# A cached-attention decode kernel: V loads follow K by one head instead of one head and one chunk, and the first loads are split over two issuing queues

## The chip, the cores and the metric

The kernel runs on one core of a Trainium2 chip. The time is the device time of the whole program in microseconds, where smaller is better. Most runs of one kernel agree within 0.3%, which is 8 us here. A program can also run in a slower, disturbed state. Engines are named TensorE (PE in the profile, PEld its weight loads), ScalarE (ACT), VectorE (DVE), GpSimd (POOL) and SyncE (SP). A "load" is a DMA of 4 MB from memory into one of four buffers.

## The reference

One token attends to a cache of 65,536 keys and values in each of 32 heads of 128 numbers (bf16). Beside it runs a small gated feed-forward network, and a scalar gate mixes the two.

```python
g = sigmoid((x * gate_w).sum(-1))
q = x @ wq                                   # 512 -> 32 heads x 128
scores = einsum(q, k_cache) * 128 ** -0.5    # 65536 scores a head
o = einsum(softmax(scores), v_cache)
a = o @ wo
b = (silu(x @ w_gate) * (x @ w_up)) @ w_down
out = g * a + (1 - g) * b
```

K and V are 512 MiB each, so each number is used once: the kernel is a stream from memory with some arithmetic behind it.

## The kernel before

K and V are cut into 128 chunks each, of 4 MB, four chunks to a head. SP loads them into a ring of four buffers in the order of `jobs`. A load may be issued only when the job four places earlier has been used up.

```python
V_LAG = 1
jobs = [("wq", i) for i in range(NQW)]
for s in range(NK):                              # NK = 128, NCH = 4
    jobs.append(("k", s))
    if s == 0:
        jobs += [("wgu", 0), ("wd", 0)]          # (cut) the feed-forward weights
    if s >= NCH + V_LAG:
        jobs.append(("v", s - NCH - V_LAG))
jobs += [("v", s) for s in range(max(0, NK - NCH - V_LAG), NK)]

@block.sync
def _(sp):
    sp.dma_start(xT, x) ...; sp.dma_start(gwT, gate_w) ...     # (cut)
    for job in jobs:
        load(sp, w, job)                         # waits until its buffer is free
```

TensorE works in slots, one for each K chunk. It transposes 96 of the chunk's 128 blocks (of 128 keys each) in 12 groups of eight, ScalarE copies each group out of PSUM (`KT`), and TensorE forms the scores; VectorE does the scores of the other 32 blocks. When a head's four chunks are done, VectorE takes the maximum, POOL reduces it over the partitions and scales it to the bias of the exponential (`nbias`), and ScalarE does one softmax piece per slot. The V chunk belonging to it is multiplied at the end of a later slot.

```python
V0 = NCH + V_LAG                                 # the slot of the first V chunk
# ScalarE, over all groups g:
if g == (V0 - 1 + n_p) * GPC + GPC // 2:         # GPC = 12: in the middle of slot V0-1+n_p
    softmax(n_p); n_p += 1
w("tdone", g + 1)                                # (cut)
nc.scalar.activation(KT[:, g % NKT, :], kt_ps(g), ACT.Copy, ...)

# TensorE
c0 = V0 + 2
for c in range(c0): slot(c, w)                   # unrolled
with nc.Fori(0, turns, 1, ...): ...              # two slots a turn
for c in range(c0 + turns * 2, NK): slot(c, w)   # the last slot
while done_v < NV:                               # the V chunks behind the last K
    if done_v in proj_at: out_proj(*proj_at[done_v])   # before V125 and before V126
    values(done_v, w); done_v += 1
w("s_otl", 1)
mm(psT[0:1, 0, 0:D], oTn[:, H - 1:H], wo_sb[:, H - 1, :], ...)    # the last head

# POOL, behind the last head's maximum and bias
w("s_rs0", 1)
nc.gpsimd.partition_all_reduce(Lt[:, 0:H - 1], rs[:, 0:H - 1], P, RADD)   # denominators of heads 0 to 30
w("s_rs1", 1)
nc.gpsimd.partition_all_reduce(Lt[:, H - 1:H], rs[:, H - 1:H], P, RADD)   # of head 31
```

ScalarE issues one more load at the start, the 4 MB output weights `wo_sb`, as 1 KB pieces. It is needed only at the end.

## Time and profile before

| Quantity | Before | Where it is read |
|---|---|---|
| Time | 2563.13 us, median of 3 runs before the prediction (2559.98 to 2563.48) | runs |
| Span of the profiled run | 2563.3 us | page |
| DMA busy | 0.9 or more in 39 of 40 slices | page, part 2 |
| Busy share of PE, ACT, DVE | 72%, 58%, 49% | page, part 1 |
| Last K chunk in (K127), first transpose | 2498.6 us | timeline |
| Wait of TensorE for the last V chunk (V127) | 1.18 us | chain of waits |

These lines are from the page of the kernel before: the DMA share and the rate in 40 slices, and the chain of work that ended last by engine.

```profile
DMA  9999999999999999999999999999999999999996
GB/s 403 423 425 432 432 431 431 430 431 430 433 430 432 430 431 433 430 433 429 433 429 431 433 426 431 430 432 427 426 425 418 431 429 427 423 422 426 422 419 297
...
DMA 67%; PE 13%; ACT 11%; issue 9%; POOL 0%; DVE 0%; ACTq 0%; SPq 0%; POOLq 0%; DVEq 0%
```

The engines that move data never rest before the last slice, and two thirds of the chain of waits is DMA. Only what moves this stream, or what comes after it, can change the time.

The start and the first head, from the timeline (start in us, duration, engine, line, operation, count; in brackets the idle time before and what ended it):

```profile
0.73 0.39 SPq L286 DMA_DIRECT2D xT<-in_A_x_dram  x1
...
1.64 0.42 SPq L252 DMA_DIRECT2D ring<-in_A_wq_dram  x1
...
19.33 3.55 PE L508 MATMUL psS<-xT,ring 128*128 128x1 bf16 x128 [12.33 <-DMA ring<-in_A_wq_dram]
...
95.84 2.30 POOL L304 PARTITION_ALL_REDUCE amx<-mxs  x1 [81.27 <-DVE mxs L441]
...
105.88 0.26 POOL L306 TENSOR_SCALAR nbias<-amx 128x1 f32<-128x1 f32 x1 [7.74 <-issue]
106.18 0.40 ACT L325 ACTIVATE pcol<-sS,nbias 128x128 bf16<-128x128 f32 x1 [5.44 <-POOL nbias L306]
...
111.05 0.33 SPq L252 DMA_DIRECT2D ring<-in_A_v_cache_dram  x1
...
123.14 0.33 SPq L252 DMA_DIRECT2D ring<-in_A_k_cache_dram  x1
```

The weights are issued third. In slot 4 ScalarE stands still for 5.44 us for the first head's bias, and the loads of V1 and K7 (111.05 and 123.14) are issued late because the buffers are still in use.

The tail is best read in the chain of waits, in order of time (start, duration, what; "issue" is time in which the profile shows no wait, here POOL's own):

```profile
2513.05 0.70 DVE mxs L441
...
2514.33 11.67 issue
...
2526.62 9.41 issue
2536.03 0.65 POOL Lt L309
...
2537.43 6.13 PE psT L596 x15
2543.56 3.31 PE psO L566 x128
2546.87 5.02 PE psT L596 x16
2551.89 3.29 PE psO L566 x128
2555.18 1.18 issue
2556.36 3.55 PE psO L566 x128
...
2560.96 0.74 DVE finrow L493
```

Behind the last head's maximum (2513.05) stand two long POOL steps (11.67 and 9.41 us), then the output projection in two parts with V125 and V126 around them. TensorE is through at 2555.18 and waits 1.18 us for V127. Two things end almost together: the stream, and the chain of work behind K127.

The trace also records 16 completions for every load. They are taken here as one from each DMA engine, which e9 and e10 bear out below; the records do not say which engine each is from. Numbered from 0 in the order of `jobs`, load 258 is V127's first part. The spread between a load's first and last completion grows from 2.5 us at load 0 to 16 us at the end. Of load 257, twelve completions come within 2.8 us, and the last comes 6.6 us after the one before it: one engine lags most. Stretches of the tail show it too (stretch, its length, busy time and count of PE, PEld, DVE, ACT, POOL; then the clock that TensorE was granted, as a share of full speed, the DMA share and GB/s):

```profile
2550.00:2555.00 5.00, 5.00 (x136) 3.77 (x135) 0.00 (x0) 0.00 (x0) 0.00 (x0) 1.00 0.07 31
```

A share of 0.07 is about one engine of 16.

### The profile page before, as it was taken

How to read it: one execution, taken by the hardware profiler on the slowest of the kernel's cores; microseconds unless marked ns; L12 is line 12 of the kernel's file. 1: busy time of each engine (PE TensorE's matmuls, PEld its weight loads, DVE VectorE, ACT ScalarE, POOL GpSimd, SP SyncE). 2: the span in 40 equal slices, each digit the busy share in tenths (PEclk: the TensorE clock that was granted, in tenths of full speed). 3: DMA queues.
4: the chain of work that ended last, by engine and by line, in shares of the span. 5: the costliest groups of instructions: out<-in, count | busy, mean ns of one | idle time of the engine just before them, and what ended most of it. 6: DMA issues, size and time to landing. Idle time of an engine off the chain costs nothing.

```text
span 2563.3 us, 88371 instructions
## 1 busy us (share of the span) xinstructions
PE 1848.0 (72%) x41279; PEld 1701.2 (66%) x41280; DVE 1259.2 (49%) x953; ACT 1484.7 (58%) x1799; POOL 42.3 (2%) x72
## 2 busy tenths in 40 slices
PE   6877777777777767776777677777766776777766
PEld 4777666666666666666766666666666666666665
DVE  2754554554455445544554454455444544455441
ACT  3766665566556655655665566556655665566552
POOL 0000000000000000000000000000000000000000
PEclk8778776777767767777676677777777777777776
DMA  9999999999999999999999999999999999999996
GB/s 403 423 425 432 432 431 431 430 431 430 433 430 432 430 431 433 430 433 429 433 429 431 433 426 431 430 432 427 426 425 418 431 429 427 423 422 426 422 419 297
DMA packets 42053, 1088.43 MB, mean 425 GB/s; under 512 B 4481, under 2 KB 8578, under 8 KB 8706
## 3 DMA queue, kind: packets, MB, share of 16 engines
q1 hardware_dynamic: 37874, 1083.46, 98.8%
q10 hardware_dynamic: 4112, 4.19, 0.5%
q8 instruction: 27, 0.44, 0.1%
q14 instruction: 40, 0.33, 0.0%
HBM read 1087.64 MB, written 0.00 MB: 424 GB/s over the span
## 4 chain that ended last, share of the span: by engine, by line
DMA 67%; PE 13%; ACT 11%; issue 9%; POOL 0%; DVE 0%; ACTq 0%; SPq 0%; POOLq 0%; DVEq 0%
DMA ring<-in_A_k_cache_dram 66%; ACT KT L345 10%; PE psT L535 9%; PE psS L548 2%; PE psO L566 1%; ACT pcol L325 1%; DMA ring<-in_A_wq_dram 1%; PE psT L596 0%; PE psT L515 0%; POOL amx L304 0%; PE psS L508 0%; PE psO L589 0%; DVE mxs L441 0%; ACTq L205 0%; DVE sS L434 0%
## 5 line engine op out<-in xcount | busy, mean ns | idle before, releaser
L345 ACT ACTIVATE KT<-psT 128x1024 bf16<-128x1024 bf16 x1536 | 1443.0, 1039 | 972.7 <-PE psT L535 969.8
L535 PE MATMUL psT<-ident,ring 128*128 128x128 bf16 x12288 | 1138.7, 255 | 527.6 <-DMA ring<-in_A_k_cache_dram 525.5
L535 PEld LDWEIGHTS psT<-ident,ring 128*128 128x128 bf16 x12288 | 912.3, 116 | 538.3 <-DMA ring<-in_A_k_cache_dram 271.7
L424 DVE TENSOR_TENSOR prod<-ring,qbc 128x2048 f32<-128x2048 bf16 x256 | 586.7, 2292 | 592.1 <-DMA ring<-in_A_k_cache_dram 586.7
L548 PE MATMUL psS<-qc,KT 128*128 128x1 bf16 x12288 | 550.8, 166 | 139.9 <-ACT KT L345 92.7
L548 PEld LDWEIGHTS psS<-qc,KT 128*128 128x128 bf16 x12288 | 467.7, 100 | 257.7 <-ACT KT L345 252.5
L426 DVE TENSOR_REDUCE sS<-prod 128x16 f32<-128x2048 f32 x256 | 585.2, 2286 | 8.7
L566 PE MATMUL psO<-pcol,ring 128*128 128x1 bf16 x16384 | 475.7, 164 | 19.9 <-issue 9.2
L566 PEld LDWEIGHTS psO<-pcol,ring 128*128 128x128 bf16 x16384 | 450.4, 99 | 24.0 <-issue 14.6
L434 DVE COPY sS<-psS 128x96 f32<-128x96 f32 x128 | 33.0, 257 | 607.2 <-PE psS L548 607.2
L325 ACT ACTIVATE pcol<-sS,nbias 128x128 bf16<-128x128 f32 x128 | 52.3, 408 | 41.7 <-POOL nbias L306 41.6
L304 POOL PARTITION_ALL_REDUCE amx<-mxs x32 | 16.1, 502 | 2137.5 <-DVE mxs L441 2137.5
L445 DVE COPY oparts<-psO 128x1 f32<-128x1 f32 x127 | 18.9, 149 | 25.2 <-PE psO L566 25.1
L306 POOL TENSOR_SCALAR nbias<-amx 128x1 f32<-128x1 f32 x32 | 24.5, 767 | 333.6 <-issue 333.6
L325 ACT ACTIVATION_READ_ACCUMULATOR pcol<-sS,nbias 128x1 f32 x128 | 26.1, 204 | 0.0
L380 DVE COPY qc<-qTb 128x1 bf16<-128x1 bf16 x128 | 19.9, 156 | 4.4
L441 DVE TENSOR_REDUCE mxs<-sS 128x1 f32<-128x512 f32 x32 | 21.7, 677 | 0.0
L332 ACT ACTIVATE qbc<-psT 128x512 bf16<-128x512 f32 x4 | 2.4, 597 | 23.1 <-PE psT L515 23.1
L596 PE MATMUL psT<-wo_sb,oTn 128*1 128x512 bf16 x31 | 11.2, 540 | 5.6 <-DVE oTn L476 5.6
L508 PE MATMUL psS<-xT,ring 128*128 128x1 bf16 x128 | 3.6, 165 | 12.3 <-DMA ring<-in_A_wq_dram 12.3
L508 PEld LDWEIGHTS psS<-xT,ring 128*128 128x128 bf16 x128 | 3.5, 104 | 12.4 <-issue 12.4
L596 PEld LDWEIGHTS psT<-wo_sb,oTn 128*1 128x1 bf16 x31 | 3.3, 110 | 12.7 <-issue 11.7
(44 smaller groups left out, 43.2 us busy)
## 6 DMA issues: line engine op xcount, KB each, us to landing
ring<-in_A_k_cache_dram SPq DMA_DIRECT2D x128, 4096.0 KB, 28.0
ring<-in_A_v_cache_dram SPq DMA_DIRECT2D x127, 4096.0 KB, 33.7
wo_sb<-in_A_wo_dram ACTq DMA_DIRECT2D x1, 4096.0 KB, 157.0
ring<-in_A_wq_dram SPq DMA_DIRECT2D x1, 4096.0 KB, 17.6
ring<-in_A_v_cache_dram SPq DMA_DIRECT2D x1, 3584.0 KB, 34.6
ring<-in_B_w_gate_dram SPq DMA_DIRECT2D x1, 1792.0 KB, 31.3
ring<-in_B_w_up_dram SPq DMA_DIRECT2D x1, 1792.0 KB, 35.5
ring<-in_B_w_down_dram SPq DMA_DIRECT2D x1, 1792.0 KB, 39.7
```

Source lines behind the costliest of these rows:

```text
L306: nc.gpsimd.tensor_scalar_mul(nbias[:, h:h + 1], amx[:, h:h + 1], -SCALE).then_inc(sm["s_nb"], 1)
L325: nc.scalar.activation(p_of(c), sS[:, h % NS, j * CB:(j + 1) * CB], ACT.Exp, bias=nbias[:, h:h + 1], scale=SCALE, accum_out=rsum[:, c:c + ...
L345: nc.scalar.activation(KT[:, g % NKT, :], kt_ps(g), ACT.Copy, bias=0.0).then_inc(sm[ev_of(g)[0]], 1)
L380: nc.vector.tensor_copy(qc[:, c % 2:c % 2 + 1], qTb[:, c // NCH:c // NCH + 1]).then_inc(sm[cq_of(c)[0]], 1)
L424: nc.vector.tensor_tensor(prod[:], kb, qb, ALU.mult).then_inc(sm["s_tt"], 1)
L426: nc.vector.reduce_sum(sS[:, h % NS, cc * CB + b0:cc * CB + b0 + DB], prod[:], AX_X).then_inc(sm["s_rd"], 1)
L434: nc.vector.tensor_copy(sS[:, h % NS, cc * CB:cc * CB + CBT], psS[:, c % 2, 0:CBT]).then_inc(sm["s_rc"], 1)
L441: nc.vector.reduce_max(mxs[:, h:h + 1], sS[:, h % NS, :], AX_X).then_inc(sm["s_mx"], 1)
L445: nc.vector.tensor_copy(oparts[:, c:c + 1], psO[:, c % 2, 0:1]).then_inc(sm[oc_of(c)[0]], 1)
L535: last = nc.tensor.transpose(dst[:, k * 128:(k + 1) * 128], src[:, b * 128:(b + 1) * 128], ident[:])
L548: last = mm(psS[:, c % 2, col:col + 1], KT[:, g % NKT, k * 128:(k + 1) * 128], qc[:, c % 2:c % 2 + 1], start=True, stop=True)
L566: last = mm(psO[:, c % 2, 0:1], src[:, b * 128:(b + 1) * 128], p_of(c)[:, b:b + 1], start=(b == 0), stop=(b == CB - 1))
```

## The change

V follows K by exactly one head (`V_LAG = 0`), so that a V chunk is multiplied in the same slot in which its softmax is done; the softmax is therefore placed at group 8 of that slot. TensorE's loop starts at slot 4 and covers every K. SP starts with the weights; x and the gate vector come by ScalarE's queue, ahead of the output weights. The gate's product, its sigmoid and the scalars move from the start into the feed-forward part.

```diff
-V_LAG = 1
+V_LAG = 0
...
 def _(sp):
-    sp.dma_start(xT[:, 0:Dc], A_x...)
-    sp.dma_start(gwT[:, 0:Dc], gate_w...)
     for job in jobs:
...
 def _(act):
+    act.dma_start(xT[:, 0:Dc], A_x...)
+    act.dma_start(gwT[:, 0:Dc], gate_w...)
     act.dma_start(wo_sb[:], wo_dram)
...
-    if g == (V0 - 1 + n_p) * GPC + GPC // 2:
+    if g == (V0 + n_p) * GPC + 2 * GPC // 3:
         softmax(n_p)
...
-            c0 = V0 + 2
+            c0 = V0
...                                   # (cut: the gate's instructions moved, the waits of the loop)
```

More of the change, by code (lines that the diff above doesn't have):

```diff
@@ L270, in __call__ @@
             def __call__(self, name, value):
-                if value > self.seen.get(name, 0):
+                if value > self.seen.get(name, -1):
                     self.seen[name] = value
@@ L285, in _ @@
             w = Waits(sp)
-            sp.dma_start(xT[:, 0:Dc], A_x.rearrange("a b (p c) -> p (a b c)", p=P)).then_inc(sm["s_x"], 16)
-            sp.dma_start(gwT[:, 0:Dc], gate_w.rearrange("(p c) -> p c", p=P)).then_inc(sm["s_gw"], 16)
             for job in jobs:
@@ L315, in _ @@
             w = Waits(act)
+            act.dma_start(xT[:, 0:Dc], A_x.rearrange("a b (p c) -> p (a b c)", p=P)).then_inc(sm["s_x"], 16)
+            act.dma_start(gwT[:, 0:Dc], gate_w.rearrange("(p c) -> p c", p=P)).then_inc(sm["s_gw"], 16)
             act.dma_start(wo_sb[:], wo_dram).then_inc(sm["s_wo"], 16)
-            w("s_z", 1)
-            nc.scalar.activation(sc[0:1, 1:2], psS[0:1, 0, 0:1], ACT.Exp, scale=-1.0).then_inc(sm["s_e1"], 1)
             def softmax(c):
@@ L335, in _ @@
                 if g == FFN_G + 2:
+                    w("s_z", 1)
+                    nc.scalar.activation(sc[0:1, 1:2], psO[0:1, 1, 64:65], ACT.Exp, scale=-1.0).then_inc(sm["s_e1"], 1)
                     w("s_h", 1)
@@ L364, in _ @@
             nc.vector.tensor_copy(xb[:], xT[:, 0:Dc].unsqueeze(2).broadcast_to([P, Dc, 128])).then_inc(sm["s_xb"], 1)
-            w("s_gw", 16)
-            nc.vector.tensor_tensor_reduce(out=zj[:, 0:Dc], in0=xT[:, 0:Dc], in1=gwT[:, 0:Dc],
-                                           scale=1.0, scalar=0.0, op0=ALU.mult, op1=ALU.add,
-                                           accum_out=zc[:, 0:1]).then_inc(sm["s_zc"], 1)
-            w("s_e1", 1)
-            chain(nc.vector.tensor_scalar_add(sc[0:1, 2:3], sc[0:1, 1:2], 1.0))
-            settle()
-            chain(nc.vector.reciprocal(sc[0:1, 3:4], sc[0:1, 2:3]))
-            settle()
-            chain(nc.vector.tensor_scalar(sc[0:1, 4:5], sc[0:1, 3:4], -1.0, 1.0, ALU.mult, ALU.add))
             w("s_q", 1)
@@ L387, in _ @@
                 nc.vector.tensor_copy(dst, src).then_inc(sm["s_qd"], 1)
+            w("s_gw", 16)
+            nc.vector.tensor_tensor_reduce(out=zj[:, 0:Dc], in0=xT[:, 0:Dc], in1=gwT[:, 0:Dc],
+                                           scale=1.0, scalar=0.0, op0=ALU.mult, op1=ALU.add,
+                                           accum_out=zc[:, 0:1]).then_inc(sm["s_zc"], 1)
             def ffn():
+                w("s_e1", 1)
+                chain(nc.vector.tensor_scalar_add(sc[0:1, 2:3], sc[0:1, 1:2], 1.0))
+                settle()
+                chain(nc.vector.reciprocal(sc[0:1, 3:4], sc[0:1, 2:3]))
+                settle()
+                chain(nc.vector.tensor_scalar(sc[0:1, 4:5], sc[0:1, 3:4], -1.0, 1.0, ALU.mult, ALU.add))
                 w("s_sig", 1)
@@ L500, in _ @@
             w("s_ones", 1)
-            w("s_zc", 1)
-            mm(psS[0:1, 0, 0:1], zc[:, 0:1], ones[:, 0:1], start=True, stop=True).then_inc(sm["s_z"], 1)
             w("s_xb", 1)
@@ L542, in scores @@
                     w(*cq_of(c))
-                    if c == 0:
-                        w("s_e1", 1)
                 w(*ev_of(g))
@@ L556, in values @@
                     w.job(("v", c))
-                    if c >= 2:
-                        w(*oc_of(c - 2))
-                    if c == 0:
-                        w("s_brow", 1)
+                    w(*oc_of(c - 2))
                 src = flat(("v", c))
@@ L571, in ffn_in @@
             def ffn_in():
+                w("s_zc", 1)
+                mm(psO[0:1, 1, 64:65], zc[:, 0:1], ones[:, 0:1], start=True, stop=True).then_inc(sm["s_z"], 1)
                 w.job(("wg" if SPLIT else "wgu", 0))
@@ L614, in slot @@
                     values(v, w)
-            c0 = V0 + 2
-            turns = max(0, (NK - c0) // 2)
-            for c in range(c0 if turns else NK):
+            c0 = V0
+            turns = (NK - c0) // 2
+            for c in range(c0):
                 slot(c, w)
-            if turns:
-                for c in range(V0, NK - 2):
-                    assert where["k", c][0] == where["k", c + 2][0]
-                    assert where["v", c - V0][0] == where["v", c + 2 - V0][0]
-                with nc.Fori(0, turns, 1, engines=bass.OrderedEngineSet([pe.engine]),
-                             hint_back_edge=True) as turn:
-                    wl = LoopWaits(pe, turn)
-                    for c in range(c0, c0 + 2):
-                        slot(c, wl)
-                w = Waits(pe)
-                for c in range(c0 + turns * 2, NK):
-                    slot(c, w)
+            w("s_brow", 1)
+            for c in range(V0, NK - 2):
+                assert where["k", c][0] == where["k", c + 2][0]
+                assert where["v", c - V0][0] == where["v", c + 2 - V0][0]
+            with nc.Fori(0, turns, 1, engines=bass.OrderedEngineSet([pe.engine]), hint_back_edge=True) as turn:
+                wl = LoopWaits(pe, turn)
+                for c in range(c0, c0 + 2):
+                    slot(c, wl)
+            w = Waits(pe)
+            for c in range(c0 + turns * 2, NK):
+                slot(c, w)
             done_v = (NK - V0) * VPC
```

## The prediction

> **What bounds the kernel now.** The page gives the 16 DMA engines 0.9 or more in 39 of 40 slices: 1083 MB at about 430 GB/s. TensorE (72%), ScalarE (58%) and VectorE (49%) wait for K; the chain of waits is 66% K transfers. The steady state, a K and a V load in 19.5 us against about 16 us of compute, is not touched. What can move is the start and the tail.
>
> **Start.** SP's first weight load is issued at 1.64 us, behind x (0.39 us of issue) and gate (0.41); it moves up by about 0.9 us. The Trainium skill, "DMA: Bandwidth & Descriptors", section "Issuing engines are not separate DMA queues", says that a second issuing engine saves only issue time; I expect no more. x lands later, but is needed only with the weights, at 19.3 us.
> In the K-only stretch (K1 to K4) a slot costs about 12.5 us (12 KT copies of 1.04 us), its load 10.1, so the four-buffer ring fills. The first head's maximum goes to POOL at 95.8; the scale behind it starts at 105.9. ScalarE, holding the softmax at group 6 of slot 4, stands still 5.4 us, and TensorE's transposes with it (6.0). V1's load is issued only at 111.0, K7's at 123.1; these landings take 11.7 and 11.5 us instead of 10.1: about 3 us lost. After the change the softmax sits at group 8, behind every copy that the transposes need, and V0 is consumed in slot 4: the ring should not run dry. Gain of the stream: about 4 us.
> Moving the gate product and sigmoid, and starting the loop at slot 4[...], takes nothing off the critical path.
>
> **Tail.** Two things end nearly together. The last V lands at 2556.2 (DMA share 0.07 from 2551 to 2555: one of 16 engines straggles). The compute chain from the last K, by the timeline: K127 in at 2498.6; maximum to POOL 2513.9; scale done 2526.3 (POOL's 12 us); softmax to 2528; denominators reduced at 2536.7 (another 10); output projection 6.1, V125 3.4, projection 5.0, V126 3.4: TensorE ends at 2555.2 and waits 1.2 us for V127. That is the slack. With V_LAG = 0, K127 moves one load (9.8 us) later in the stream. From K127's landing to the end is 63.5 us without that wait (an estimate from those durations); from V127's landing, 7. After: K127 lands at 2508.5 - 4 = 2504.5, plus 63.5 = 2568. The last V, in at about 2552, waits for TensorE. The tail costs about 8.6 us and the start returns 4.
>
> **Predicted:** 2567 us, 4 us slower (0.2%); eight in ten between 2558 and 2574. Faster by over 2%: 0.01; within 2%: 0.97; slower by over 2%: 0.02.
>
> **What would show it.** Right: first weight load near 0.7 us; no landings 11.5 us apart near 115 to 140; ACT's wait for nbias in slot 4 about 3 us; K127's transposes from about 2504; no wait for V127; DMA idle over the last 15 us. Wrong: TensorE still waiting for V127 at the end.
>
> **What would make it wrong.** If the straggling engine's own work changes, the stream shifts by some us; if POOL's gaps in the tail are shorter than 12 and 10 us, the tail costs less; if the early stall is not cured because V0 must be finished inside slot 4, the 3 us are not returned.

## The result, and the profile after

The changed kernel takes 2572.68 us (median of 4 runs, 2570.61 to 2575.36), against 2562.34 us (4 runs) of the kernel before. The ratio is 1.0042, with a 95% interval from 1.0025 to 1.006. Ratios here and below are the mean time of one kernel's fast runs over that of the other's of the same rounds, so not quite the ratio of the medians. The change cost about 10 us, 0.4%. The traced run of the changed kernel is its fastest (2570.61 us) and that of the kernel before is longer than its median (2565.06 us), so the two traces differ by 5.5 us only.

The rate over 40 slices, from the page of the changed kernel:

```profile
GB/s 405 424 429 428 430 431 431 432 430 431 432 429 431 432 431 431 432 432 428 432 433 429 432 429 432 429 429 429 417 424 421 431 420 427 422 423 424 425 419 270
```

In the mean it is the rate of before; the last slice, in which the stream is over, is lower (270 against 297). The start after, from the timeline:

```profile
0.72 0.39 SPq L252 DMA_DIRECT2D ring<-in_A_wq_dram  x1
...
14.61 0.43 DVE L363 COPY xb<-xT 128x512 bf16<-128x512 bf16 x1 [13.75 <-DMA xT<-in_A_x_dram]
...
15.14 3.55 PE L506 MATMUL psS<-xT,ring 128*128 128x1 bf16 x128 [15.14 <-DVE xb L363]
...
100.25 0.26 POOL L304 TENSOR_SCALAR nbias<-amx 128x1 f32<-128x1 f32 x1 [7.29 <-issue]
100.54 0.40 ACT L322 ACTIVATE pcol<-sS,nbias 128x128 bf16<-128x128 f32 x1 [2.59 <-POOL nbias L304]
...
103.28 0.33 SPq L252 DMA_DIRECT2D ring<-in_A_k_cache_dram  x1
```

The weights go out at 0.72 us and TensorE begins at 15.14 us, 4.2 us earlier than before. The weights have landed by 14.4 us instead of 19.2; TensorE now waits for x, which came at 14.6 us, by the queue that shares the engines with the weights. ScalarE's wait for the bias falls from 5.44 to 2.59 us, and the next load that was late before (load 11) goes out at 103.28 instead of 111.05. All of this was as intended, and none of it lasted. The next table has the last of the 16 completions of some loads, in us from the start of the span, from the traces:

| Load | 10 | 11 | 12 | 29 | 40 | 128 | 200 | 258 (V127) | Span |
|---|---|---|---|---|---|---|---|---|---|
| Before | 115.4 | 127.0 | 138.5 | 305.2 | 412.1 | 1275.3 | 1984.6 | 2556.3 | 2563.3 |
| After | 111.5 | 121.9 | 132.1 | 304.5 | 412.0 | 1275.3 | 1985.4 | 2557.9 | 2568.8 |

At load 12 the changed kernel is 6.4 us ahead; at load 40 it is 0.1 us ahead. Over the first 400 us both traces show the same rate (stretch of the kernel before, then of the changed one; the last number is GB/s):

```profile
0.00:400.00 400.00, 294.57 (x6165) 265.95 (x6167) 207.14 (x162) 239.60 (x286) 9.94 (x16) 0.78 1.00 425
```

```profile
0.00:400.00 400.00, 289.48 (x6175) 260.77 (x6176) 200.16 (x159) 233.30 (x279) 5.54 (x15) 0.76 1.00 425
```

The tail after, as a chain of waits:

```profile
2523.89 0.70 DVE mxs L441
...
2525.16 10.61 issue
...
2536.38 8.96 issue
2545.34 0.65 POOL Lt L307
...
2546.74 5.31 PE psT L591 x15
2552.05 3.29 PE psO L559 x128
2555.34 3.54 PE psT L591 x16
2558.88 6.57 PE psO L559 x256
...
2566.51 0.74 DVE finrow L493
```

The last head's maximum comes 10.8 us later (2523.89 against 2513.05), because K127 is one place later in the stream. Behind it stands the same chain. TensorE does V126 and V127 in one piece (6.57 us at 2558.88) with no wait between them: V127 was in at 2557.9 (its first part; the rest at 2559.1), and the chain, not the stream, ends last.

### The profile page after: what moved, and what is told of

It reads as the page before. It is cut to its first block, busy times and chain, and to the rows that moved or that the text cites. A ratio compares the mean times of both kernels' runs of the same rounds, so it can differ in the third digit from the quotient of the medians.

```text
span 2568.8 us, 88385 instructions
## 1 busy us (share of the span) xinstructions
PE 1838.6 (72%) x41279; PEld 1692.2 (66%) x41280; DVE 1259.1 (49%) x953; ACT 1481.8 (58%) x1799; POOL 33.6 (1%) x72
## 4 chain that ended last, share of the span: by engine, by line
DMA 69%; PE 13%; issue 10%; ACT 7%; DVE 0%; POOL 0%; ACTq 0%; POOLq 0%; DVEq 0%; SPq 0%
DMA ring<-in_A_k_cache_dram 68%; PE psT L533 10%; ACT KT L344 7%; PE psS L544 2%; ACT pcol L322 1%; PE psO L559 1%; DMA xT<-in_A_x_dram 1%; PE psT L591 0%; PE psT L513 0%; PE psS L506 0%; PE psO L584 0%; POOL amx L302 0%; ACTq L205 0%; DVE mxs L441 0%; DVE finrow L493 0%
## 5 line engine op out<-in xcount | busy, mean ns | idle before, releaser
L304 POOL TENSOR_SCALAR nbias<-amx 128x1 f32<-128x1 f32 x32 | 17.8, 556 | 329.5 <-issue 329.5
```

Source lines behind the costliest of these rows:

```text
L304: nc.gpsimd.tensor_scalar_mul(nbias[:, h:h + 1], amx[:, h:h + 1], -SCALE).then_inc(sm["s_nb"], 1)
```

## The experiments

The theory after the result was that V_LAG = 0 causes the loss: K127 comes one load later and the chain behind it no longer fits behind the last V loads. The rivals were the queues (x, gate and output weights beside the first loads) and the loop (register waits from the fifth slot on). Each kernel was timed in five rounds beside the kernel before (its median was 2560.4 to 2562.4 us); all results were correct.

| Run | What it is | Median us | Ratio to before, 95% interval |
|---|---|---|---|
| e1_lag_only | before with V_LAG = 0 | 2570.80 | 1.0037 (1.0023 to 1.0051) |
| e2_queue_only | before with the queues changed | 2562.86 | 1.0012 (0.9999 to 1.0026) |
| e3_after_lag1 | changed, with V_LAG = 1 | 2562.12 | 1.0005 (0.9991 to 1.0019) |
| e4_after_early | changed, chain behind K127 shortened | 2566.53 | 1.0021 (1.0008 to 1.0035) |
| e5_before_early | before, the same shortening | 2560.73 | 0.9995 (0.9982 to 1.0009) |
| e6_lag2 | before with V_LAG = 2 | 2565.05 | 1.0008 (0.9994 to 1.0021) |
| e7_before_wo_late | before, output weights at slot 30 | 2570.73 | 1.0032 (1.0019 to 1.0046) |
| e8_after_wo_late | changed, output weights at slot 30 | 2571.59 | 1.0037 (1.0023 to 1.0051) |
| e9_relief120 | e5, three V loads cut 120 + 8 | 2625.49 | 1.0259 (1.0245 to 1.0273) |
| e10_relief104 | e5, three V loads cut 104 + 24 | 2632.97 | 1.0283 (1.0268 to 1.0298) |
| e11_lag0_early | e1 with the shortening | 2564.51 | 1.0018 (1.0005 to 1.0032) |
| e12_early_tail40 | e5, V127 cut 88 + 40 blocks | 2559.68 | 0.9987 (0.9974 to 1.0000) |

### One part alone, and one part undone: e1, e2, e3

```diff
 # e1: the kernel before
-V_LAG = 1
+V_LAG = 0
-    if g == (V0 - 1 + n_p) * GPC + GPC // 2:
+    if g == (V0 + n_p) * GPC + 2 * GPC // 3:
 # e2: the kernel before; the two small loads go from SP to ScalarE's queue
-    sp.dma_start(xT...); sp.dma_start(gwT...)
+    act.dma_start(xT...); act.dma_start(gwT...)        # ahead of wo_sb
 # e3: the changed kernel
-V_LAG = 0
+V_LAG = 1
-    if g == (V0 + n_p) * GPC + 2 * GPC // 3:
+    if g == (V0 - 1 + n_p) * GPC + GPC // 2:
```

> The kernel before with V_LAG = 0 and the softmax moved to group 8 of the same slot, nothing else of the change. Tail theory (K127 lands one load later and the chain behind it then ends last): the whole slowdown, 2568 to 2573 us, no wait of TensorE for V127. Queue theory (the slowdown is in the start: x, gate and the output weights beside the first loads): no change, 2560 to 2564. Loop theory (the register waits from the fifth slot cost TensorE): no change either, since the loop begins two slots after the first V here as before.

> The kernel before with x and gate moved to ScalarE's queue ahead of the output weights, nothing else. Tail theory: within 2 us of before (2560 to 2564), because the last K and V land when they did. Queue theory: 2568 to 2573. My prediction's own sub-claim, that the first weight load 0.9 us earlier moves the stream by 0.9 us, would give 2561.5.

> The changed kernel with V_LAG = 1 and the softmax back in the middle of the slot before, everything else as changed (queues, place of the gate, loop from the first V slot). Tail theory: back to 2560 to 2564. Queue or loop theory: stays at 2568 to 2573.

The lag alone gives 1.0037, nearly all of the whole change's 1.0042. With the lag undone the changed kernel is at 1.0005, level with the kernel before; its loop still starts at the first V slot, so the loop is cleared, and most of the queue's suspicion falls with it. e2's 1.0012 has an interval that just reaches 1, so a small cost of the queues (at most some 6 us by its upper end) is not excluded by this run; e3, which has the same queues, does not show it. My sub-claim of 0.9 us gained by the earlier weights did not show in either. In the chain of waits of e1 the last line of V work is one piece of two chunks, as in the changed kernel:

```profile
2552.15 5.05 PE psT L596 x16
2557.20 6.62 PE psO L566 x256
```

The traces agree on where the end comes from. Where TensorE waits for V127 (before, e2 to e7, e9 to e11), the span ends 7.0 us after V127's landing. In the three with V_LAG = 0 and the long chain it ends later: 10.9 us after it in the changed kernel, 12.9 in e1 and 15.6 in e8. So the chain costs 3.9, 5.9 and 8.6 us in these single traces.

### Taking the chain behind K127 apart: e4, e5, e11

These take POOL's second long step and the output projection out of the chain, without removing a wait from anything: the denominators of heads 0 to 30 do not need K127, so VectorE sums them before it scores the last chunk, POOL reduces them before the last maximum, and TensorE projects those heads ahead of V124 and V125.

```diff
 # POOL
 for h in range(H):
+    if h == H - 1:
+        w("s_rs0", 1)
+        nc.gpsimd.partition_all_reduce(Lt[:, 0:H - 1], rs[:, 0:H - 1], P, RADD).then_inc(sm["s_l0"], 1)
     w("s_mx", h + 1)
...
-w("s_rs0", 1)
-nc.gpsimd.partition_all_reduce(Lt[:, 0:H - 1], ...)       # was behind the last bias
 # VectorE, in the last slot, ahead of scored(c)
+    w(*ex_of(NK - NCH - 1)); w(*ex_of(NK - NCH - 2))
+    nc.vector.reduce_sum(rs[:, 0:H - 1], ...).then_inc(sm["s_rs0"], 1)
 # TensorE
-first = max(done_v, (H - 1) * NCH * VPC, NV - 3 * VPC)
+first = max(done_v, (H - 1) * NCH * VPC)
```

> The changed kernel with the denominators of heads 0 to 30 reduced on POOL before the last head's maximum, and the output projection of those heads ahead of V124: takes one 10 us POOL gap and about 9 us of TensorE work out of the chain behind K127. Tail theory: TensorE waits for V127 again and the end is V127's landing plus 7 us, about 4 us less than the changed kernel (2567 to 2569), not less. If the chain behind K127 were the whole of the 10 us, it would be 2562. Queue and loop theories: no change, 2571 to 2574.

> The kernel before (V_LAG = 1) with the denominators of heads 0 to 30 reduced ahead of the last head's maximum and their projection ahead of V124. Tail theory: the kernel before ends with V127's landing and had only 1.2 us of slack in the chain behind K127, so this is worth at most 1 us: 2560 to 2562. If the chain behind K127 bounded the kernel before as well, 3 to 6 us: 2556 to 2559.

> The kernel before with V_LAG = 0 (as e1) and the early denominators: the chain behind K127 no longer ends last, and x and gate are on SP's queue as before. e4 (the same with all of the change) was 5 us over the kernel before, e5 (V_LAG = 1) 1.3 us under it. If the rest of the slowdown, apart from the chain behind K127, comes with V_LAG alone: 2565 to 2568, as e4. If it comes from the queues or the loop: 2560 to 2562, as e5.

The same edit is worth 5.4 us in the changed kernel (1.0042 - 1.0021, of 2562 us; a difference of two ratios, so with an uncertainty of 3 to 5 us) and 1.3 us in the kernel before (1.0000 - 0.9995), which is not clear of noise. Nothing is what one expects there: its profile showed TensorE waiting 1.18 us for V127, so the chain did not end last and shortening it can't help. The chain of waits of e4 shows why the edit is worth no more there: TensorE waits for V127 again.

```profile
2545.91 6.77 PE psO L560 x256
2552.68 4.39 issue
2557.07 3.56 PE psO L560 x128
```

The 4.39 us between V126 and V127 are the stream's. So the chain is no longer last in e4, and yet e4 is 5 us over the kernel before. e11 has V_LAG = 0 and the same shortening, but the old queues and the old start of the loop: 1.0018, as e4. The rest of the loss therefore comes with V_LAG too, and it sits in the stream. In the single traces of e5 and e11 the landings agree up to load 200 (1981.6 and 1981.9 us), and load 257 comes at 2541.5 and 2545.1: 9.82 and 9.88 us a load in that stretch. The three other traces with V_LAG = 0 and early output weights (after, e1, e4) have 9.89 to 9.92 there, the three others with V_LAG = 1 (before, e2, e3) 9.84 to 9.88, where the 9.88 is the kernel before's, whose traced run was a long one. With the output weights late the two are nearly level (e8, V_LAG = 0: 9.85; e7, V_LAG = 1: 9.83). That is a tendency, not a cause. It is not a wait for a buffer: from load 200 on, every load of all these traces is issued at least 14 us before the load ahead of it has its last completion. What slows the last fifth of the stream stays open.

### A longer lag: e6

```diff
-V_LAG = 1
+V_LAG = 2
```

> The kernel before with V_LAG = 2: K127 one load earlier still. Tail theory alone: more slack behind K127, the end still V127's landing plus 7 us, so no change from before (2560 to 2563). Rival, from e4 (bound by V127 again and yet about 4 us over the kernel before): a shorter lag makes the transfers themselves slower in the second half; then a longer one should make them faster, 2556 to 2559.

It was 2565.05 us, 1.0008, not separable from the kernel before. TensorE waits 5.15 us for V127, so there is more slack behind K127, as the theory has it, and that slack buys nothing. The rival, that a longer lag makes the stream faster, is not borne out: the time is not below that of before, and the trace has 9.92 us a load after load 200, as with V_LAG = 0.

### Where the gain at the start went: e7, e8

My prediction had counted the late landings at 115 to 140 us as lost time. The table of landings says that nothing was lost. The theory was that the engines used the pause of SP's queue for the output weights, which have to be moved at some time anyway. Both kernels were run with those moved out of the way.

```diff
-act.dma_start(wo_sb[:], wo_dram).then_inc(sm["s_wo"], 16)     # at the start
...
 for g in range(NG):
+    if g == 30 * GPC:
+        act.dma_start(wo_sb[:], wo_dram).then_inc(sm["s_wo"], 16)
```

> The kernel before with the 4 MB of output weights loaded by ScalarE at slot 30 instead of at the start. My prediction counted 3 us of lost stream at 115 to 140 us in the kernel before. Theory now: the engines were not idle there, they moved output weights, so nothing was lost. With those moved away the dry stretch costs: landing number 29 comes 2 to 4 us later than in the next run, and the time is 2563 to 2566. If the dry stretch costs nothing even then, the time is that of before and both runs' landings agree.

> The changed kernel with the output weights loaded at slot 30. It has no dry stretch, so moving the output weights away takes nothing from it: 2570 to 2574, as the changed kernel; its landing number 29 comes 2 to 4 us before that of the run before.

Stretches of e7, then of e8 (DMA share and GB/s are the last two numbers):

```profile
80.00:120.00 40.00, 25.65 (x470) 22.03 (x468) 24.70 (x16) 27.86 (x35) 2.56 (x2) 0.79 0.89 369
```

```profile
80.00:120.00 40.00, 29.86 (x635) 26.27 (x632) 24.88 (x16) 29.01 (x35) 2.56 (x2) 0.83 1.00 425
```

Without the output weights the engines of the kernel before do stand still in that stretch (share 0.89, 369 GB/s), and those of the changed kernel do not (1.00, 425). At load 10 the two are level (107.5 and 107.2 us); load 29 lands at 299.4 in e7 and 293.5 in e8: the dry stretch costs 5.9 us, more than the 2 to 4 expected. In the times, the kernel before loses 8 us by this edit (1.0032) and the changed kernel nothing (1.0037 against 1.0042). That settles it: the dry stretch was real, the changed order does cure it, and the cure was worth nothing because the pause had been filled. The pages of the kernel before and of the changed one show the filling too; the last number is the time from issue to landing of the output weights:

```profile
wo_sb<-in_A_wo_dram ACTq DMA_DIRECT2D x1, 4096.0 KB, 157.0
```

```profile
wo_sb<-in_A_wo_dram ACTq DMA_DIRECT2D x1, 4096.0 KB, 299.2
```

Without the pause the same 4 MB take until 300.8 us instead of 157.8. e7 also shows that loading the output weights at the start is a good choice of the kernel before.

### Relieving the lagging engine, a failure: e9, e10

The end of the kernel before waits for one engine of 16, so a few loads were cut so that the highest-numbered engine (e9) or the highest three (e10) should get no part of them. The Trainium skill, "DMA: Bandwidth & Descriptors", section "Why a DMA increments its semaphore by 16 and not by 1", says that a transfer issued from SyncE or ScalarE uses the lowest-numbered k engines, where k is the largest number up to 16 that divides the size of the slowest dimension of both sides, here the partitions. The traces agree as to how many engines: of the small parts, 8 partitions (e9) post 8 completions and 24 (e10) post 12, and of the large ones 120 post 15 and 104 post 13, each with one more record within about 1 us of the issue. Which engines they are, no run shows.

```diff
+RELIEF = (0, 1, NK - 3)
+RROWS = 120                                       # e10: 104
 def pieces(job):
+    if kind == "v" and i in RELIEF:
+        return [(dst[0:RROWS], src[0:RROWS]), (dst[RROWS:P], src[RROWS:P])]
```

> The kernel before with the early denominators of e5, and three V loads (V0, V1, V125) split in two transfers of 120 and 8 partitions. The Trainium skill, DMA: Bandwidth & Descriptors, says that a transfer of 120 partitions uses the 15 lowest-numbered of the 16 DMA engines, and one of 8 partitions the 8 lowest. One engine finishes every load last, by up to 17 us at the end. If that straggler is the engine left out, its work falls by three times 9.7 us, the spread of the landings ends below 10 us and the time is 2545 to 2555. If another engine is the straggler, the time is that of e5 or up to 4 us more, 2560 to 2565, and the spread at the end stays near 16 us.

> The same with 104 and 24 partitions: by the same page engines 0 to 12 and 0 to 11, so the three highest-numbered engines are relieved and the others get 7 us more in all. If the straggler is one of the two engines next to the last, this run is faster (2548 to 2557) and e9 is not. If it is the last engine, both are faster, this one less, by the 3 to 4 us more that the others carry. If neither, 2562 to 2570.

With a semaphore for each small part both ran, and they were 2.6 and 2.8% slower. Two stretches of e9, one before and one within the cut loads:

```profile
70.00:80.00 10.00, 8.33 (x167) 6.56 (x165) 9.83 (x8) 10.00 (x12) 0.00 (x0) 1.00 1.02 430
...
140.00:150.00 10.00, 8.05 (x157) 7.06 (x155) 6.96 (x4) 10.00 (x13) 0.00 (x0) 0.90 1.03 214
```

The engines are counted busy (1.03), but move 214 GB/s instead of 430. So the part of 120 partitions moves at half the rate, and the expectation had no term for that. The small parts cost too: the two cut loads at the start put load 12 back by 34 us (171.1 us against 137.4 in e5), where half the rate for two loads alone would be 20 us (an estimate from 10 us a load). The runs say nothing of a gain by relief. They do say one thing of the straggler in e9: by load 14 one engine is far ahead (first completion at 174.6, second at 184.4, last at 191.4 us), while the last completion's lag behind the ninth of the 16 still grows, from 4.0 us at load 14 to 12.0 at load 128, about as in the kernel before (1.1 to 9.9). If the one ahead is the relieved one, as it seems, another lags; which, and why, stays open.

### A try at a version that beats both: e12

```diff
 # e5, and
-TAIL = 16
+TAIL = 40            # blocks of V127 that come in its second part
```

> A try at a version faster than both kernels: the kernel before with the early denominators of e5 and, as the end is V127's landing plus 7 us, V127 cut so that 40 of its 128 blocks come in the second transfer instead of 16. TensorE then does 88 blocks (2.4 us) while the last 40 are still on their way (3 us at 0.076 us a block) and has 1.1 us left after them: an estimate of 1.2 us less than e5 and about 2.5 us less than before, 2558 to 2560. If the second transfer comes no sooner after the first than before, or the straggling engine brings both late, no change from e5 (2560 to 2562).

e12 takes 2559.68 us, against 2562.44 of the kernel before in the same rounds: 0.9987 (0.9974 to 1.0000), about 3 us less, at the edge of what five rounds can tell, and 13 us below the changed kernel's median.

```profile
2550.66 2.49 PE L567 MATMUL psO<-pcol,ring 128*128 128x1 bf16 x88 [3.10 <-issue]
...
2553.67 1.23 PE L567 MATMUL psO<-pcol,ring 128*128 128x1 bf16 x40 [0.53 <-DMA ring<-in_A_v_cache_dram]
```

TensorE does 88 blocks as soon as the first part is in, then waits 0.53 us for the second and needs 1.23 us for it. In the kernel before, 3.55 us of V127 work came after the first part. Against the changed kernel the gain is clear; against the kernel before it is not shown beyond doubt, and the share of e5's edit in it was not measured apart.

## Why the prediction was right or wrong

- **The time.** 2567 us was predicted, in 2558 to 2574; 2572.68 was measured. The sign was right and the size was off: 4 us of loss predicted, about 10 measured. That 2572.68 still lies in the range is partly luck: a gain of 4 us that was worth nothing and a loss of some 5 us in the stream that was not foreseen add up, and the tail, set at 8.6, came out smaller.
- **What bounds the kernel.** Right. Stream and chain behind K127 ended within 1.2 us of each other, and the steady state did not move: load 128 lands at 1275.3 us in both.
- **The tail as the cause.** Right in mechanism. K127's transposes start later, TensorE does not wait for V127, and e4 gets 5.4 us back by shortening that chain. The estimate was 8.6 us. In the trace the chain from K127's transposes (2510.03) to the end took 58.8 us, not 63.5: POOL's steps were 10.61 and 8.96 us instead of 11.67 and 9.41, and the projection 5.31 and 3.54 us instead of 6.13 and 5.02. For the second part the granted clock was 0.71 in those 5 us before and 1.00 in those 3.6 us after; the Trainium skill, "TensorE: Matmul & The Clock Gate", section "Part 1: The HAM clock gate", says that the array's clock is gated by how busy it has been of late, and the clock did differ here, but these numbers do not show that as the reason: TensorE had been busy without a gap for 9.4 us before the one stretch (from 2537.43) and for 8.6 us before the other (from 2546.74). I had taken the durations of the tail before as fixed. With V127 in at 2557.9 and 7 us behind it, this trace's own cost of the chain is 2568.8 - 2564.9, about 4 us; in e1 it is 5.9 and in e8 8.6, so the 8.6 of the prediction is at the upper end of what the traces show.
- **"Gain of the stream: about 4 us".** This is the step that failed. The observations were right (ScalarE's wait was 2.59 us, about 3 predicted; no landings 11.5 us apart; weights at 0.72 us), but the term was worth nothing: by load 40 the lead was 0.1 us. The late landings were counted as idle engines, though the DMA share in the profile before stayed at 1.0 there. e7 and e8 show what filled the pause.
- **A term that was missing.** V_LAG = 0 also makes the stream end later, 4.6 us by e11 (1.0018) when the chain is out of the way. Nothing in the prediction has it; its cause is open.
- **The sum.** Predicted 8.6 - 4. Measured, by ratios: 5.4 for the chain and 5.4 for the rest (e4 over before).
- **Queues, gate and loop start off the critical path.** Not contradicted: e3, with all of them and V_LAG = 1, is at 1.0005. x was not as harmless as I wrote, for it lands at 14.6 us, 0.2 us behind the weights, and TensorE waits for it; by load 40 nothing of that is left.
- **K127's transposes at about 2504, DMA idle for the last 15 us.** Both wrong, by the stream: 2510.03, and 10.9 us from V127's landing to the end.

## What to carry to other kernels

In a kernel bound by a stream, look at the order of the last loads: what has the longest chain of work behind it should land first, and the slack is the end of the stream minus the end of that chain, to be read in the chain of waits. A pause in one queue costs only if no other transfer that is due anyway can use it; read the DMA share and the bytes of that stretch, not the distance of one queue's landings. Before taking out a wait, ask what ends just after it: e5 won nothing clear of noise (1.3 us) where e4 won 5 by the same edit.

## What the Trainium skill lacked or had wrong

- "DMA: Bandwidth & Descriptors", section "Issuing engines are not separate DMA queues", says that transfers from several issuing engines run on the same 16 engines and interleave, and that only issue time is saved. These runs agree for the whole stream (load 40 at 412.1 and 412.0 us). It has no figure for the other side: a tiny transfer beside large ones gets slow. x (1 KB) landed 1.7 us after its issue when ahead of the weights on SP's queue, and 13.9 us after it on ScalarE's queue beside them (8.7 to 9.0 us in e2, e3, e4 and e8).
- The same page, section "Why a DMA increments its semaphore by 16 and not by 1", lets one work out how many engines a transfer of 120 partitions uses, but no page has a figure for its rate: 214 GB/s in e9 against 430 for the loads of 128 partitions.
- The same page, section "Latency and other measured facts", ties slower engines, as a best guess, to transfers described by software. Here all loads come from SP and ScalarE, and still one engine falls behind by up to 17 us in 258 loads (DMA share 0.07 from 2550 to 2555 us).
- "GPSIMD Engine Reference", section "2.1 Instruction dispatch", gives about 6 us for the first call after new code is loaded, with no visible instruction. Between the reduction and the bias the profile before has 333.6 us in 32 times, 10.4 us each, every time and not only the first. The trace has two MODIFY_POOL_CONFIG instructions, the mark from which the page counts, ahead of each of these 32 steps (64 at L306), so here the code seems to be loaded anew at every change of operation: reduction and bias alternate. The two reductions in a row at the end have none between them, and only 0.78 us. What the page lacks is that alternating costs this each time, and the size here, 7.74 to 12.45 us.
